# A weight gradient computed transposed: 240 matmuls of 512 columns for 384 of 320, with a round trip through DRAM to turn the result back

## The chip, the cores and the metric

The kernel runs on one core of a Trainium2 chip. The metric is device time in microseconds (us), from repeated executions; a profile of one execution gives a span that is about 2 us shorter than its time.

## The reference

A two-layer MLP with a SiLU in the middle, forward and backward, in bf16:

```python
B, S, D, F = 1, 2048, 640, 1536
def _fwd_reference(x, w1, w2):
    h = silu(einsum("bsd,df->bsf", x, w1))
    return einsum("bsf,fd->bsd", h, w2)
# outputs: out, and the gradients gx, gw1, gw2 for a given grad_out
```

The part of interest is gw2 = aᵀ · grad_out, with a = silu(x·w1): a matrix of 1536 x 640, summed over 2048 rows. gw1 is the same kind of product: xᵀ · gh.

## The kernel before

The main phase runs over four chunks of 512 rows. In each it makes `aT` and `ghT` (features on partitions), writes both to DRAM scratch, and computes `out` and `gx` from them. The final phase needs `a` and `gh` with rows on partitions, so it reads the scratch back through transposing DMAs. All DMAs are issued from SyncE, on one queue, in order. A matmul is written with a stationary operand (`lhsT`, put in place by a weight load) and a moving one (`rhs`), whose columns are counted below. Its sums go to PSUM tiles; an eviction is the copy of a finished tile from PSUM to on-chip memory by ScalarE or VectorE.

```python
    ps_h = ctx.enter_context(tc.tile_pool(name="ps_h", bufs=4, space=bass.MemoryType.PSUM))
    ps_o = ctx.enter_context(tc.tile_pool(name="ps_o", bufs=2, space=bass.MemoryType.PSUM))
    ...
    def load_a_blk(ft, pool):                       # one block of 128 features
        a_blk = pool.tile([P, ST, P], dt_in, name="a_blk")
        nc.sync.dma_start_transpose(out=a_blk[:], in_=aT_scr[ft * P:(ft + 1) * P, :])
        a_blks.append(a_blk)
    ...                                             # main phase; its last chunk loads blocks 0 to 3
        ab2pool = fctx.enter_context(tc.tile_pool(name="ab2pool", bufs=FT - NAB))
        for ft in range(NAB, FT):                   # blocks 4 to 11, in memory that the main phase frees
            load_a_blk(ft, ab2pool)
        for fc in range(NFC):                       # then three gh blocks of 512 features
            gh_blk = gbpool.tile([P, ST, FC], dt_in, name="gh_blk")
            nc.sync.dma_start_transpose(out=gh_blk[:], in_=ghT_scr[fc * FC:(fc + 1) * FC, :])
            ...
        for ft in range(FT):                        # gw2: 12 x 2 x 16 matmuls, 320 moving columns
            a_blk = a_blks[ft]
            op_ = ps_o.tile([P, 2, 512], FP32, name="op")
            for hf in range(2):
                for st in range(ST):
                    nc.tensor.matmul(op_[:, hf, 0:DH], lhsT=a_blk[:, st, :],
                                     rhs=go_nat[:, st, hf * DH:(hf + 1) * DH], ...)
            nc.scalar.activation(gw2_sb[:, ft, :]..., op_[:, :, 0:DH], ACT.Copy)
        nc.sync.dma_start(out=gw2..., in_=gw2_sb[:])
        for fc in range(NFC):                       # gw1: 3 x 5 x 16 matmuls, 512 moving columns
            ...
```

## Time and profile before

323.03 us, median of 3 runs (323.01 to 323.51). The page of the profile, first the busy time of engines, then rows of the timeline (each digit is the busy tenths of one of 40 slices), then the chain that ended last (what the end of the kernel waited for, followed backwards), by engine:

```profile
PE 316.2 (98%) x1926; PEld 188.5 (59%) x1944; DVE 99.1 (31%) x172; ACT 78.9 (25%) x136; POOL 0.7 (0%) x6
...
PE   8999999999999999999999999999999999999996
...
DMA  7999999998794020291020079909999996211111
...
PE 97%; DMA 1%; issue 0%; DVE 0%; DVEq 0%
```

TensorE (PE) is busy in every slice and is 97% of the chain. VectorE (DVE) and ScalarE (ACT) are at a third or less. The DMA engines have idle stretches, the last at the end, during gw1.

The groups of gw2 and gw1 (line, engine, operation, output and input; count; then busy us and mean ns of one; then idle time before):

```profile
L263 PE MATMUL op<-go_nat,a_blk 128*128 128x320 bf16 x384 | 52.3, 299 | 0.0
L302 PE MATMUL hp<-gh_blk,x_nat 128*128 128x512 bf16 x219 | 48.2, 379 | 0.3
L263 PEld LDWEIGHTS <-a_blk 128*128 128x128 bf16 x384 | 37.5, 98 | 14.7
```

The 299 and 379 ns are durations of overlapping instructions, not the rate. The rate is read from the chain in order of time (start us, length us, what):

```profile
214.43 52.16 PE op L263 x384
...
266.86 10.74 PE hp L302 x49
...
277.65 10.74 PE hp L302 x49
...
318.52 0.29 DVE g_2755 L295
```

gw2 is one piece of 52.16 us: 52.16 / 384 = 135.8 ns a matmul. The gw1 pieces are 49 recorded matmuls (one record of fifty is missing), and start 277.65 - 266.86 = 10.79 us apart: 215.8 ns a matmul. The spacing of starts is called the pitch below. The last line is the last eviction.

The DMA issues of the final phase, in order of time (start us, length us, line, kind, what):

```profile
193.06 10.97 SPq L73 DMA_TRANSPOSE a_blk<-aT_scr  x4
204.13 0.53 SPq L192 DMA_DIRECT2D out_dram<-o_sb  x1
214.46 2.01 SPq L73 DMA_TRANSPOSE a_blk<-aT_scr  x1
216.53 0.57 SPq L192 DMA_DIRECT2D out_dram<-o_sb  x1
217.15 19.33 SPq L73 DMA_TRANSPOSE a_blk<-aT_scr  x7
236.53 26.25 SPq L254 DMA_TRANSPOSE gh_blk<-ghT_scr  x3
```

The fifth block of a is issued only when the main phase's last matmul has freed its memory, and the queue is then full until 262.8 us.

### The profile page before, as it was taken

To read this page: it belongs to the slowest core of one execution; us is meant where nothing else is said; L and a number is where in the kernel's file an instruction comes from. 1 tells how busy PE (TensorE), PEld (TensorE's weight loads), DVE (VectorE), ACT (ScalarE), POOL (GpSimd) and SP (SyncE) were. 2 spreads that over 40 slices of the span, in tenths; PEclk is the share of its full clock that TensorE was granted. 3 is DMA by queue.
4 is the path that set the end of the run, shared out by engine and by line. 5 is a ranking of instruction groups with operands and counts; after the bars stand their busy time and mean duration, and the time that the engine had idled before them with its cause. 6 is when DMAs were issued, how large, how long until landed. Compare 5 with 4: busy or idle time off the path is not lost.

```text
span 321.2 us, 4386 instructions
## 1 busy us (share of the span) xinstructions
PE 316.2 (98%) x1926; PEld 188.5 (59%) x1944; DVE 99.1 (31%) x172; ACT 78.9 (25%) x136; POOL 0.7 (0%) x6
## 2 busy tenths in 40 slices
PE   8999999999999999999999999999999999999996
PEld 6467457544577644477754467777777775444443
DVE  1860553577501287800357740220000000110001
ACT  3961000455210155411044521001111111000100
POOL 0000000000000000000000000000000000000000
PEclk9999999999999999999999999999999999999999
DMA  7999999998794020291020079909999996211111
GB/s 235 318 191 200 220 274 241 363 289 274 213 290 137 6 78 0 78 316 67 17 82 0 0 254 245 239 17 236 226 218 213 266 219 211 85 38 44 35 42 41
DMA packets 113731, 52.32 MB, mean 163 GB/s; under 512 B 84144, under 2 KB 113712, under 8 KB 113712
## 3 DMA queue, kind: packets, MB, share of 16 engines
q1 hardware_dynamic: 113712, 52.04, 64.1%
q8 instruction: 15, 0.25, 0.3%
q14 instruction: 4, 0.03, 0.0%
HBM read 9.18 MB, written 21.76 MB: 96 GB/s over the span
## 4 chain that ended last, share of the span: by engine, by line
PE 97%; DMA 1%; issue 0%; DVE 0%; DVEq 0%
PE op L180 32%; PE op L263 16%; PE hp L163 16%; PE hp L144 16%; PE hp L302 15%; DMA x_nat<-in_x_dram 1%; PE hp L284 1%; PE tp L118 0%; DVE g_2755 L295 0%; DVEq L295 0%
## 5 line engine op out<-in xcount | busy, mean ns | idle before, releaser
L144 PE MATMUL hp<-xT,w_nat 128*128 128x512 bf16 x229 | 56.3, 379 | 0.6
L163 PE MATMUL hp<-goT,w2T 128*128 128x512 bf16 x238 | 56.8, 379 | 0.1
L180 PE MATMUL op<-w1T,ghT 128*128 128x320 bf16 x384 | 52.8, 299 | 0.0
L180 PE MATMUL op<-w_nat,aT 128*128 128x320 bf16 x384 | 52.8, 299 | 0.0
L263 PE MATMUL op<-go_nat,a_blk 128*128 128x320 bf16 x384 | 52.3, 299 | 0.0
L151 ACT ACTIVATE aT<-hp 128x512 bf16<-128x512 f32 x48 | 28.7, 597 | 83.0 <-PE hp L144 83.0
L302 PE MATMUL hp<-gh_blk,x_nat 128*128 128x512 bf16 x219 | 48.2, 379 | 0.3
L180 PEld LDWEIGHTS <-aT 128*128 128x128 bf16 x384 | 37.5, 98 | 15.3
L180 PEld LDWEIGHTS <-ghT 128*128 128x128 bf16 x384 | 37.5, 98 | 14.8
L263 PEld LDWEIGHTS <-a_blk 128*128 128x128 bf16 x384 | 37.5, 98 | 14.7
L163 PEld LDWEIGHTS <-w2T 128*128 128x128 bf16 x240 | 23.5, 98 | 28.2
L144 PEld LDWEIGHTS <-w_nat 128*128 128x128 bf16 x240 | 23.4, 98 | 27.8
L170 DVE SCALAR_TENSOR_TENSOR ghT<-ghT,hp 128x512 bf16<-128x512 bf16 x48 | 32.5, 682 | 16.2 <-PE hp L163 16.2
L191 DVE CAST o_sb<-op 128x640 bf16<-128x640 f32 x16 | 13.2, 825 | 78.6 <-PE op L180 78.6
L302 PEld LDWEIGHTS <-x_nat 128*128 128x128 bf16 x224 | 21.9, 98 | 26.3
L156 DVE SCALAR_TENSOR_TENSOR ghT<-aT,v 128x512 bf16<-128x512 bf16 x48 | 33.0, 687 | 0.6
L153 ACT ACTIVATE t<-hp 128x512 f32<-128x512 f32 x48 | 28.4, 592 | 0.0
L155 DVE TENSOR_SCALAR v<-t 128x512 bf16<-128x512 f32 x48 | 20.5, 427 | 20.5 <-ACT t L153 20.5
L189 ACT ACTIVATE o_sb<-op 128x640 bf16<-128x640 f32 x16 | 11.2, 703 | 49.1 <-PE op L180 49.1
L270 ACT ACTIVATE gw_sb<-op 128x640 bf16<-128x640 f32 x12 | 8.4, 704 | 56.8 <-PE op L263 56.8
L313 DVE CAST g_2475<-hp 128x512 bf16<-128x512 f32 x1 | 0.7, 690 | 58.2 <-PE hp L302 58.2
L90 PE MATMUL wp<-warm 128*128 128x128 bf16 x36 | 3.8, 304 | 1.0 <-DVE warm L85 1.0
(31 smaller groups left out, 26.2 us busy)
## 6 DMA issues: line engine op xcount, KB each, us to landing
aT_scr<-aT SPq DMA_DIRECT2D x4, 1536.0 KB, 6.3
ghT_scr<-ghT SPq DMA_DIRECT2D x4, 1536.0 KB, 9.6
out_dram<-o_sb SPq DMA_DIRECT2D x8, 640.0 KB, 4.4
x_nat<-in_x_dram SPq DMA_DIRECT2D x4, 640.0 KB, 5.4
go_nat<-in_grad_out_dram SPq DMA_DIRECT2D x4, 640.0 KB, 7.0
w_nat<-in_w_dram SPq DMA_DIRECT2D x2, 960.0 KB, 11.5
out_dram<-gw_sb SPq DMA_DIRECT2D x1, 1920.0 KB, 6.9
w_nat<-in_w_dram SPq DMA_DIRECT2D x2, 640.0 KB, 7.6
```

The lines of the kernel that those rows point to most:

```text
L144: nc.tensor.matmul(hp[:], lhsT=w1_nat[:, dt_, ft * P:(ft + 1) * P], rhs=xT[:, dt_, :], start=(dt_ == 0), stop=(dt_ == DT - 1),)
L151: nc.scalar.activation(aT[:, ft, :], hp[:], ACT.Silu)
L153: nc.scalar.activation(t[:], hp[:], ACT.Tanh, scale=0.5)
L155: nc.vector.tensor_scalar(out=v[:], in0=t[:], scalar1=-0.5, scalar2=0.5, op0=ALU.mult, op1=ALU.add)
L156: nc.vector.scalar_tensor_tensor(out=ghT[:, ft, :], in0=aT[:, ft, :], scalar=1.0, in1=v[:], op0=ALU.subtract, op1=ALU.mult)
L163: nc.tensor.matmul(gp[:], lhsT=w2T[:, dt_, ft * P:(ft + 1) * P], rhs=goT[:, dt_, :], start=(dt_ == 0), stop=(dt_ == DT - 1),)
L170: nc.vector.scalar_tensor_tensor(out=ghT[:, ft, :], in0=ghT[:, ft, :], scalar=1.0, in1=gp[:], op0=ALU.add, op1=ALU.mult)
L180: nc.tensor.matmul(op_[:, hf, 0:DH], lhsT=lhs_all[:, ft, sl * P:(sl + 1) * P], rhs=rhs_all[:, ft, hf * DH:(hf + 1) * DH], start=(ft == 0), ...
L189: nc.scalar.activation(dst, op_[:, :, 0:DH], ACT.Copy)
L191: nc.vector.tensor_copy(out=dst, in_=op_[:, :, 0:DH])
L263: nc.tensor.matmul(op_[:, hf, 0:DH], lhsT=a_blk[:, st, :], rhs=go_nat[:, st, hf * DH:(hf + 1) * DH], start=(st == 0), stop=(st == ST - 1),)
L302: nc.tensor.matmul(gp[:], lhsT=x_nat[:, st, dt_ * P:(dt_ + 1) * P], rhs=gh_blk[:, st, :], start=(st == 0), stop=(st == ST - 1),)
```

## The change

The intent: gw2 streams 320 columns a matmul, because 640 is split in two. With the operands swapped (grad_out stationary, a moving) it streams 512, as gw1 does, in fewer matmuls and fewer weight loads. The result is then gw2ᵀ, which is written to a DRAM scratch, read back through a transposing DMA and stored. Loads of a become three blocks of 512 features. Core of the diff, with cuts:

```diff
-    abpool = ctx.enter_context(tc.tile_pool(name="abpool", bufs=NAB))
+    abpool = ctx.enter_context(tc.tile_pool(name="abpool", bufs=1))
+    g2T_scr = dram.tile([D, F], dt_in, name="g2T_scr")
-    def load_a_blk(ft, pool):
-        a_blk = pool.tile([P, ST, P], dt_in, name="a_blk")
+    def load_a_blk(fc, pool):
+        a_blk = pool.tile([P, ST, FC], dt_in, name="a_blk")
 ...
-        fpool = fctx.enter_context(tc.tile_pool(name="fpool", bufs=1))
+        fpool = fctx.enter_context(tc.tile_pool(name="fpool", bufs=NFC))
 ...
+        for fc in range(NFC):
+            a_blk = a_blks[fc]
+            g2T = fpool.tile([P, DT, FC], dt_in, name="g2T")
+            for dt_ in range(DT):
+                gp = ps_h.tile([P, FC], FP32, name="hp")
                 for st in range(ST):
                     nc.tensor.matmul(
+                        gp[:],
+                        lhsT=go_nat[:, st, dt_ * P:(dt_ + 1) * P],
+                        rhs=a_blk[:, st, :],
 ...
+                if k % 2 == 0:
+                    nc.scalar.activation(g2T[:, dt_, :], gp[:], ACT.Copy)
+                else:
+                    nc.vector.tensor_copy(out=g2T[:, dt_, :], in_=gp[:])
+            nc.sync.dma_start(out=g2T_v[:, :, fc * FC:(fc + 1) * FC], in_=g2T[:])
+        def store_gw2(fc):
+            g2 = fpool.tile([P, FB, D], dt_in, name="g2")
+            nc.sync.dma_start_transpose(out=g2[:], in_=g2T_scr[:, fc * FC:(fc + 1) * FC])
+            nc.sync.dma_start(out=gw2_v[:, fc * FB:(fc + 1) * FB, :], in_=g2[:])
 ...                                                # gw1 loop:
+                if dt_ == DT // 2:
+                    store_gw2(fc)
```

## The prediction

> **What bounds the kernel now.** TensorE, end to end. The page's first part has PE busy 98% of the 321.2 us span, the chain that ended last is 97% PE, and the granted clock is 1.000 (cores view). In the chain in order of time the gw2 stage is one piece: 384 matmuls in 52.16 us, 135.8 ns each, from 214.43 us, waiting for nothing. In the gw1 stage behind it (512 moving columns) pieces of 50 matmuls start 10.79 us apart: 215.8 ns each. Weight loads (98 ns each) hide under both. VectorE (31%) and ScalarE (25%) are far from a limit.
>
> **TensorE.** The columns streamed are equal: 384 x 320 = 240 x 512. From the two pitches one column costs (215.8 - 135.8) / 192 = 0.4167 ns and one matmul 2.5 ns beside its columns. That agrees with the Trainium skill, page "TensorE: Matmul & The Clock Gate", section "Wait — 56ns, not 53.3ns?": N / 2.4 GHz + about 2.5 ns when warm. The new stage costs 240 x 215.8 = 51.8 us, 0.36 us less: 144 matmuls fewer at 2.5 ns. The 144 fewer weight loads (14 us of PEld) were hidden and give nothing. That 0.36 us is on the critical path and is the whole gain.
>
> **Added, off the path.**
> - Evictions: 15 of 128x512 (0.60 us ScalarE, 0.69 us VectorE) for 12 of 128x640 (0.70 us). A PSUM tile fills in 3.45 us and has four buffers: no stall.
> - Loads of a: three transposing DMAs of 2 MB for twelve of 0.5 MB. The gh loads have this form: about 8.75 us of queue time, 11.3 us to landing. The second block can be issued only when main-phase buffers come free, at about 214.5 us (queue's waits: so it was for the fifth small block). Estimate: it lands near 226 us, needed at 214.4 + 17.3 = 231.7. The third lands near 236, needed at 249; the gh blocks end near 262, as before.
> - gw2 round trip: 1.9 MB written, transposed back, stored. The queue issues in order, so the first two scratch writes wait behind the gh loads (to about 260 us); the third trip falls near 267 to 283 us, where the DMA engines are 21% busy (windows view). gw1 stores wait some us behind it; three g1 buffers and four of PSUM cover that. All is over some 35 us before the end; the last gw1 tile and its store are unchanged.
>
> **Prediction.** 323.03 - 0.36 = 322.7 us; range 322.0 to 323.7. Faster by over 2%: 0.01; within 2%: 0.97; slower by over 2%: 0.02.
>
> **What the profile would show.** Right: the chain still 97% PE; gw2 in one piece of about 51.8 us at 215.8 ns, gw1 starting 0.4 us earlier; PEld down from 59% to about 54%; no PE wait on DMA at block boundaries; the scratch transposes landed before 290 us; tail equal. Wrong: a PE wait of some us near 231.7 us for the second a block; idle PE in gw1 released by ScalarE or VectorE (gw1 stores held up in the queue); the chain ending on a DMA of gw2.
>
> **What would make it wrong.** The second a block landing over 6 us later than estimated (a wait on a later buffer, DMA engines shared with the output store); the transposing read of the scratch far slower than the 5.9 us that equal-sized transposes of x took; a lower granted clock.

## The result and the profile after

322.58 us, median of 4 runs (322.52 to 322.96), against 323.27 us of the kernel before in all its 4 runs. The ratio is 0.998, with a 95% interval of 0.9963 to 0.9997: within 2%, and 0.69 us between the medians. Ratios here are the mean time of one kernel's runs over that of the other's of the same rounds, so not quite the ratio of the medians quoted. Executions over 1.5% slower than the fastest of the same kernel are left out of the means.

The same parts of the page, after:

```profile
PE 317.0 (99%) x1800; PEld 174.9 (55%) x1800; DVE 104.0 (32%) x179; ACT 75.3 (23%) x132; POOL 0.7 (0%) x6
...
PE   8999999999999999999999999999999999999996
...
DMA  7999999997795020191020079809999999851011
...
PE 98%; DMA 1%; DVE 0%; issue 0%; DVEq 0%
```

Still TensorE from end to end. Weight loads went down by four points of the span, and the DMA row is busy for two slices more.

The group and the chain in order of time, after:

```profile
L266 PE MATMUL hp<-a_blk,go_nat 128*128 128x512 bf16 x240 | 52.0, 379 | 0.0
...
L266 PEld LDWEIGHTS <-go_nat 128*128 128x128 bf16 x240 | 23.5, 98 | 28.2
```

```profile
214.48 51.80 PE hp L266 x240
266.28 48.35 PE hp L314 x224
314.63 3.51 PE hp L296 x32
...
318.21 0.29 DVE g_2613 L307
```

gw2 takes 51.80 us, 0.36 us less than 52.16, and gw1 follows without a gap. The DMA issues of the final phase, after:

```profile
192.88 10.32 SPq L73 DMA_TRANSPOSE a_blk<-aT_scr  x1
203.29 0.53 SPq L192 DMA_DIRECT2D out_dram<-o_sb  x1
214.51 7.51 SPq L73 DMA_TRANSPOSE a_blk<-aT_scr  x1
222.07 0.57 SPq L192 DMA_DIRECT2D out_dram<-o_sb  x1
222.70 10.54 SPq L73 DMA_TRANSPOSE a_blk<-aT_scr  x1
233.28 25.43 SPq L253 DMA_TRANSPOSE gh_blk<-ghT_scr  x3
258.88 1.02 SPq L278 DMA_DIRECT2D g2T_scr<-g2T  x2
262.47 3.76 SPq L282 DMA_TRANSPOSE g_2327<-g2T_scr  x1
...
277.02 2.73 SPq L282 DMA_TRANSPOSE g_2533<-g2T_scr  x1
...
283.29 0.38 SPq L283 DMA_DIRECT2D out_dram<-g_2533  x1
```

The second block of a was issued at 214.51 us, and its issue-to-landing time in the view of that tile is 9.6 us: it was there at 224.1 us, needed at 214.48 + 80 x 0.2158 = 231.7. The first two gw2 tiles wait for the queue until 258.88 us, behind the gh loads, though the first was complete at about 232 us. The third trip ends near 287 us, over 30 us before the end.

**What was left over.** The medians differ by 0.69 us and the stage by 0.36. The profiles let one separate what the change did from what varies anyway. Call A the start of the first matmul on the chunk's data (the end of the twenty transposes of x at the start), B the start of gw2, and C the end of the last eviction. A is the start of this piece of TensorE's timeline, before and after:

```profile
6.35 5.99 PE L144 MATMUL hp<-xT,w_nat 128*128 128x512 bf16 x26
```

```profile
6.40 5.77 PE L144 MATMUL hp<-xT,w_nat 128*128 128x512 bf16 x26
```

| run | A | A to B | B to C |
|---|---|---|---|
| before | 6.35 | 208.08 | 104.38 |
| after | 6.40 | 208.08 | 104.02 |
| after, second profile | 6.86 | 208.08 | 104.02 |

From A to C nothing varies by more than 0.01 us between these runs, except for what the change did: 0.36 us. What varies lies outside. A went from 6.35 to 7.13 us over all the profiles, and the time from C to the end of the span from 2.29 to 2.56 us (the kernel with gw2 last, which ends differently, left aside). The spans of the first two profiles differ by 0.42 us: 0.36 from B to C, 0.11 less after C, and 0.05 more before A. One run of each comparison has a trace, so that the rest of the 0.69 us between the medians lies before A or after C too is inferred.

### The profile page after: what moved, and what is told of

It reads as the page before. It is cut to its first block, busy times and chain, and to the rows that moved or that the text cites. A ratio compares the mean times of both kernels' runs of the same rounds, so it can differ in the third digit from the quotient of the medians.

```text
span 320.8 us, 4127 instructions
## 1 busy us (share of the span) xinstructions
PE 317.0 (99%) x1800; PEld 174.9 (55%) x1800; DVE 104.0 (32%) x179; ACT 75.3 (23%) x132; POOL 0.7 (0%) x6
## 4 chain that ended last, share of the span: by engine, by line
PE 98%; DMA 1%; DVE 0%; issue 0%; DVEq 0%
PE op L180 33%; PE hp L144 16%; PE hp L266 16%; PE hp L163 16%; PE hp L314 15%; DMA x_nat<-in_x_dram 1%; PE hp L296 1%; PE tp L118 0%; DVE g_2613 L307 0%; DVEq L307 0%
## 5 line engine op out<-in xcount | busy, mean ns | idle before, releaser
L266 PE MATMUL hp<-a_blk,go_nat 128*128 128x512 bf16 x240 | 52.0, 379 | 0.0
L266 PEld LDWEIGHTS <-go_nat 128*128 128x128 bf16 x240 | 23.5, 98 | 28.2
L163 PEld LDWEIGHTS <-w2T 128*128 128x128 bf16 x240 | 23.5, 98 | 28.2
L191 DVE CAST o_sb<-op 128x640 bf16<-128x640 f32 x16 | 13.2, 825 | 78.6 <-PE op L180 78.6
L144 PEld LDWEIGHTS <-w_nat 128*128 128x128 bf16 x240 | 23.5, 98 | 27.7
L276 DVE CAST g2T<-hp 128x512 bf16<-128x512 f32 x7 | 4.8, 692 | 43.4 <-PE hp L266 43.4
L274 ACT ACTIVATE g2T<-hp 128x512 bf16<-128x512 f32 x8 | 4.8, 597 | 60.0 <-PE hp L266 60.0
## 6 DMA issues: line engine op xcount, KB each, us to landing
ghT_scr<-ghT SPq DMA_DIRECT2D x4, 1536.0 KB, 10.1
```

What stands on the lines that cost most here:

```text
L144: nc.tensor.matmul(hp[:], lhsT=w1_nat[:, dt_, ft * P:(ft + 1) * P], rhs=xT[:, dt_, :], start=(dt_ == 0), stop=(dt_ == DT - 1),)
L163: nc.tensor.matmul(gp[:], lhsT=w2T[:, dt_, ft * P:(ft + 1) * P], rhs=goT[:, dt_, :], start=(dt_ == 0), stop=(dt_ == DT - 1),)
L191: nc.vector.tensor_copy(out=dst, in_=op_[:, :, 0:DH])
L266: nc.tensor.matmul(gp[:], lhsT=go_nat[:, st, dt_ * P:(dt_ + 1) * P], rhs=a_blk[:, st, :], start=(st == 0), stop=(st == ST - 1),)
```

## The experiments

Eleven kernels ran. "Before" in a comparison is the old kernel on the same chip.

**The changed kernel again**, unedited, with five rounds.

> The changed kernel once more, for a sharper ratio. Theory (144 matmuls fewer at 2.5 ns, nothing else on the path): 0.36 us less than before, ratio 0.9989. Rival (part of the first 0.69 us between the medians comes from elsewhere): 0.7 us, ratio 0.998.

Measured: 323.03 us (322.49 to 323.33, 5 runs), before 323.32; ratio 0.9988, interval 0.9976 to 1.0. The ratio is within 0.0001 of the theory's 0.9989, but its interval also holds the rival's. The trace decides: A to B is as before, and B to C is again 104.02 us. In this run the start was what varied. Transposes of x, in the kernel before and in this kernel's second profile (durations as minimum, median and maximum in ns):

```profile
L118 PE MATMUL tp<-ident,x_nat x20: 215/220/230, 5.1 to 6.1; 128*128 128x128 bf16 x20
```

```profile
L118 PE MATMUL tp<-ident,x_nat x20: 219/311/311, 5.1 to 6.8; 128*128 128x128 bf16 x20
```

The twenty took 1.30 us in the first and 1.95 us in the second (timeline view). Five in a row early in the second stand as one piece of 0.74 us, so their starts are (0.74 - 0.31) / 4, about 107 ns, apart; seven in a row in the first stand as 0.55 us, (0.55 - 0.22) / 6, about 55 ns apart. The Trainium skill, page "TensorE: Matmul & The Clock Gate", section "What's actually happening", says that the array runs at half its clock until a window of about 3.4 us has been busy, that the window runs freely, and that the switch therefore falls at a different place from run to run. This agrees with what is seen here, where the switch falls before or within the transposes. It is read from durations: the granted clock of these slices is shown as 1.00 in all of these runs.

**One term at a time: columns for a matmul.** Two kernels compute gw2 as changed, but with shorter moving operands:

```diff
-                for st in range(ST):
-                    nc.tensor.matmul(gp[:], lhsT=go_nat[...], rhs=a_blk[:, st, :], ...)
+                for lo in range(0, FC, 256):          # and 128
+                    for st in range(ST):
+                        nc.tensor.matmul(gp[:, lo:lo + 256], lhsT=go_nat[...],
+                                         rhs=a_blk[:, st, lo:lo + 256], ...)
```

> The changed kernel with gw2 in 480 matmuls of 256 moving columns, all else equal. Theory (a matmul costs 0.4167 ns a column and 2.5 ns beside them, weight loads hidden): pitch 109.2 ns, gw2 stage in the chain 52.4 us against 51.8. Rival (the gain came from fewer weight loads, which show when the matmul gets near the 98 ns of a load): pitch clearly above 109.2 ns, stage above 53 us.

> The same with 960 matmuls of 128 columns. Theory: pitch 55.8 ns, gw2 stage 53.6 us, 1.8 us more than with 512 columns. Rival (loads set the pace): a load of 98 ns can't hide behind 56 ns, pitch near 98 ns, stage near 94 us.

The stage in the chain in order of time, with 256 columns and then with 128:

```profile
214.99 52.40 PE hp L267 x480
```

```profile
214.55 53.60 PE hp L267 x960
```

Both are the theory's numbers: 109.2 and 55.8 ns a matmul. (The single times, 323.71 and 324.46 against 323.15 us for before, carry the scatter of the start.) That the gain comes from weight loads too long to hide is ruled out. With 128 columns there are 960 loads of 98 ns in 53.6 us:

```profile
L267 PEld LDWEIGHTS <-go_nat 128*128 128x128 bf16 x960 | 53.7, 98 | 0.1
```

The loader is busy without a pause and still adds nothing to the pace. So its 98 ns is the length of one load, of which several overlap, and not the time between loads. One thing the runs can't separate: every matmul here has a load of its own, so the 2.5 ns belongs to the pair, and whether a matmul that keeps its weights would cost it too was not tested.

**The loads alone.** The kernel before with three big loads of a and the old matmuls:

```diff
-        a_blk = pool.tile([P, ST, P], dt_in, name="a_blk")
+        a_blk = pool.tile([P, ST, FC], dt_in, name="a_blk")
 ...
-                        lhsT=a_blk[:, st, :],
+                        lhsT=a_blk[:, st, fo:fo + P],   # fo = (ft % 4) * P
```

> The kernel before with the new loads of a alone: three transposing DMAs of 2 MB in place of twelve, gw2 still 384 matmuls of 320 columns. Theory: the loads are off the path, ratio to before 1.000 within 0.0005, gw2 stage 52.16 us, no PE wait at the block boundaries. Rival (fewer DMAs gave part of the gain): ratio 0.999 or less.

Measured: 323.48 us (322.98 to 323.92), ratio 1.0007, interval 0.9994 to 1.002. The ratio is 0.0002 outside the expected band of 0.0005 about 1, well inside its own interval. In the trace A to B is 208.08 us, gw2 is 52.16 us in one piece, B to C is 104.38 us. The loads contribute nothing.

**No round trip.** The transposed tiles are stored straight into gw2, whose content is then wrong (relative error 1.41 in that output; the other three are right):

```diff
-            nc.sync.dma_start(out=g2T_v[:, :, fc * FC:(fc + 1) * FC], in_=g2T[:])
+            nc.sync.dma_start(out=gw2_v[:, fc * FB:(fc + 1) * FB, :],
+                              in_=<g2T, flattened and cut in rows of D>)
 ...
-                if dt_ == DT // 2:
-                    store_gw2(fc)
```

> The changed kernel without the round trip: the transposed tiles are stored straight into gw2, so that output is wrong on purpose; same bytes stored, no scratch, no transposing DMA. Theory (the trip is hidden under gw1): the same time as the changed kernel, 322.6 us within 0.2. Rival (its delay of the gw1 stores or its DMA traffic costs something): 0.5 us or more faster than the changed kernel.

Measured: 323.33 us (323.15 to 323.54), which is 0.30 us above the changed kernel on the same chip (against before, ratio 1.0002, interval 0.999 to 1.0014), and so a miss of "within 0.2 of 322.6". The profiled run, at 323.54 us the slowest of the five, shows nothing of the trip: it has A = 7.13 us, the latest of all, and 2.50 us after C against 2.31, but 208.08 us from A to B and 104.02 us from B to C, equal to the changed kernel in both. The trip costs nothing, where it stands. (The other four runs have no trace; that they too are late before A or after C is inferred.)

**Where it stands.** gw1 first and gw2 last (with the first gh block loaded early in place of the first a block, and sixteen buffers for the gw1 tiles in place of three, so that they don't stall):

```diff
-        for fc in range(NFC):   # gw2, then gw1 with store_gw2(fc) inside
+        for fc in range(NFC):   # gw1, then gw2 with store_gw2(fc) at each block's end
```

> The changed kernel with gw1 computed first and gw2 last (the first gh block loaded early in place of the first a block, sixteen buffers for the gw1 tiles so that their stores can wait). Theory (the round trip costs nothing only because gw1 stands behind it): after the last matmul an eviction of 0.6 us, a scratch write of about 3.5 us, a transposing read of about 5.5 us and a store of about 3.4 us stand in line, 13 us against 2 us now: about 334 us, chain ending on these DMAs. Rival (the trip is cheap anywhere): below 326 us.

Measured: 333.24 us in one look, 10.1 us above before. The end of the timeline, from the last eviction on:

```profile
318.53 0.60 ACT L322 ACTIVATE g2T<-hp 128x512 bf16<-128x512 f32 x1 [6.31 <-PE hp L314]
319.15 0.37 SPq L326 DMA_DIRECT2D g2T_scr<-g2T  x1
322.47 2.90 SPq L301 DMA_TRANSPOSE g<-g2T_scr  x1
327.38 0.37 SPq L302 DMA_DIRECT2D out_dram<-g  x1
```

Write, transposing read and store stand in line from 319.15 us to the end of the span at 331.4. The trip that is free in front of gw1 costs some 10 us behind it.

**The buffers.** The same kernel with fewer buffers for g2T and g2:

```diff
-        fpool = fctx.enter_context(tc.tile_pool(name="fpool", bufs=NFC))
+        fpool = fctx.enter_context(tc.tile_pool(name="fpool", bufs=2))      # and bufs=1
```

> The changed kernel with two buffers in place of three for the gw2 tiles. Theory (the scratch writes queue behind the gh loads until about 259 us, so the third block's evictions wait for the first write to land near 265 us, while four PSUM tiles fill by 262.8 us): PE idle once for 2 to 3 us in the last third of gw2, time near 325.3 us. Rival (the buffers are a reserve, not needed): no idle PE, 322.6 us.

> The same with one buffer. Theory: the second block's evictions wait until the first scratch write lands near 264 us; four PSUM tiles are full at 245.6 us; PE idle about 18 us, perhaps 2 us more for a colder clock after it: 339 to 346 us. Rival: as before, below 326 us.

Measured: 324.01 us with two (325.3 expected) and 342.12 us with one (339 to 346 expected), before 323.15. TensorE in order of time, with two buffers (gw2's last two pieces):

```profile
214.75 48.51 PE L266 MATMUL hp<-a_blk,go_nat 128*128 128x512 bf16 x224
264.09 3.61 PE L266 MATMUL hp<-a_blk,go_nat 128*128 128x512 bf16 x16 [0.83 <-ACT g2T L274]
```

and with one:

```profile
214.36 31.24 PE L266 MATMUL hp<-a_blk,go_nat 128*128 128x512 bf16 x144
262.00 23.78 PE L266 MATMUL hp<-a_blk,go_nat 128*128 128x512 bf16 x96 [16.39 <-ACT g2T L274]
```

With two buffers the stall is there, in the predicted place (after 14 groups of 16 matmuls), but it is 0.83 us and not 2 to 3. What was mis-sized is the landing of the first scratch write: the expectation had it near 265 us; it landed 3.50 us after its issue, at 263.34. The changed kernel's own trace held the figure: there the three writes took 3.5 to 6.4 us, and the read that waits for the first was issued at 262.47, 3.6 us after the write. B to C is 105.01 us, 0.99 us more than with three buffers. With one buffer TensorE is idle for 16.39 us, and the 96 matmuls after it take 23.78 us in place of 96 x 0.2158 = 20.72. That second loss of 3.06 us is the clock: the granted clock of the run is 0.975, its row falls to 7, 5 and 7 tenths there, and the windows view has it at 0.50 from 252 to 266 us and at 1.00 from 268 us. The page named above, section "HAM oscillation — how this bites in real kernels", says that TensorE falls back to half its clock after idling for more than about 3.4 us; this trace agrees. So three buffers are no reserve: the first two tiles are held from about 232 and 249 us until the queue has issued the gh loads.

**The same trick elsewhere.** If 2.5 ns a matmul is all there is, it is also to be had in `out` and `gx`, which use 320 columns as well. Six of their eight phases (chunks 0 to 2) were computed transposed, each with its own trip:

```diff
+        def sdT_phase(c, mov_all, w_all, dst_v, scr, on_act):
+            oT = opool.tile([P, DT, SC], dt_in, name="oT", tag="o_sb")
+            for dt_ in range(DT):
+                gp = ps_h.tile([P, SC], FP32, name="hp")
+                for ft in range(FT):
+                    nc.tensor.matmul(gp[:], lhsT=w_all[:, ft, dt_ * P:(dt_ + 1) * P],
+                                     rhs=mov_all[:, ft, :], ...)
+                ...                                    # eviction to oT
+            nc.sync.dma_start(out=<scr, columns of chunk c>, in_=oT[:])
+            o_sb = opool.tile([P, STC, D], dt_in, name="o_sb")
+            nc.sync.dma_start_transpose(out=o_sb[:], in_=<scr, columns of chunk c>)
+            nc.sync.dma_start(out=dst_v[:, c * STC:(c + 1) * STC, :], in_=o_sb[:])
```

The tile oT shares two buffers with o_sb.

> The changed kernel with the same trick in six of the eight out and gx phases (chunks 0 to 2): 60 matmuls of 512 columns for 96 of 320, through a scratch and a transposing DMA. Theory: 216 matmuls fewer at 2.5 ns, 0.54 us less than the changed kernel if all six trips stay hidden, about 322.0 us, and 0.9 us less than before. Rival (the single queue, which also brings the next chunk's operands, makes TensorE wait): slower than the changed kernel by a microsecond or more, with PE waits at a chunk's start.

Measured: 324.07 us (322.58 to 328.04, 6 runs). The 328.04 us run is slow; the five fast ones have a median of 323.96 us, against 323.03 for the changed kernel on the same chip, and a ratio to before of 1.0023, interval 0.9994 to 1.0052. That leans to the rival's side, but the interval holds 1. The trace has the rival's wait. In the profiled run (323.19 us) A to B is 208.09 us, so that the 0.54 us are given back in full: this one phase of chunk 1 takes 13.49 us, from 97.40 to 110.89, against 60 x 0.2158 = 12.95. TensorE in chunk 1:

```profile
97.40 10.52 PE L201 MATMUL hp<-ghT,w1T 128*128 128x512 bf16 x47
108.31 2.75 PE L201 MATMUL hp<-ghT,w1T 128*128 128x512 bf16 x12 [0.39 <-DVE oT L211]
```

and the queue ahead of it:

```profile
92.33 11.46 SPq L109 DMA_TRANSPOSE goT<-in_grad_out_dram  x1
103.88 0.53 SPq L213 DMA_DIRECT2D oT_scr<-oT  x1
107.46 2.50 SPq L215 DMA_TRANSPOSE o_sb<-oT_scr  x1
```

It is the stall of the two-buffer experiment again: the write of the first tile waits behind an 11.46 us load for the next chunk, and the eviction of the next tile waits for the write. The slower unprofiled runs, 326.23 and 328.04 us with a granted clock of 0.995, have no trace; whether they are longer stalls of this kind, with a clock that falls in them as in the one-buffer run, or something else, stays open.

Two versions with a third buffer, the second one with the `out` phase of the last chunk transposed as well:

```diff
-            v = tpool.tile([P, SC], dt_in, name="v")
+            v = tpool.tile([P, SC], dt_in, name="v", bufs=2)      # makes the room
-        opool = mctx.enter_context(tc.tile_pool(name="opool", bufs=2))
+        opool = mctx.enter_context(tc.tile_pool(name="opool", bufs=3))
```

> The six transposed phases again, with three buffers in place of two for the tile tag that the transposed tile and the output tile share (room for it comes from one buffer less for a small tile that VectorE alone writes and reads). Theory (the stall of the first try was an eviction waiting for a scratch write queued behind the next chunk's loads; a third buffer takes that wait away): no PE wait on VectorE in chunk 1, from the first matmul of the main phase to the end 0.54 us less than the changed kernel, times steady, about 322.2 us. Rival (the six trips overload the one queue whatever the buffers): still PE waits and a scatter up to some us.

> The same with the out phase of the last chunk too (seven phases). Theory: a further 36 matmuls fewer, 0.09 us, if its trip ends before the second a block is issued near 214.5 us; 0.63 us less than the changed kernel. Rival: its trip delays the second or third a block past the 7 us of margin, and TensorE waits in gw2.

Measured with six phases: 322.97 us (322.7 to 323.13), ratio 0.9994, interval 0.9982 to 1.0007; with seven: 322.43 us (322.08 to 322.9), ratio 0.9977, interval 0.9964 to 0.9991; before 323.14 in both. The time of the first missed its 322.2 us, by its start and its end: A was 7.07 us against the changed kernel's 6.40, and from C on it took 2.56 us against 2.31. From A to B it took 207.54 us, which is 0.54 us less than before, and no PE wait on VectorE is left. With seven phases A was 6.72 us and A to B 207.46, 0.62 less. With the 0.36 us of gw2 that makes 0.98 us; 396 matmuls fewer at 2.5 ns are 0.99. The rival on the a blocks fails: gw2 and gw1 still take 104.02 us from B to C. This last version is the fastest by its median and by its trace. Against the changed kernel it was not timed in the same rounds; the two intervals, each against before, overlap.

## Why the prediction was right

- *"0.36 us is on the critical path and is the whole gain."* Shown. gw2 went from 52.16 to 51.80 us, A to B stayed at 208.08, and the time after C (2.42 us before, 2.31 after) is within its scatter. The measured median (322.58) is 0.1 us below the 322.7 forecast; that the time came so close is luck, as the same kernel's median was 323.03 us when it ran again and the kernel before had 323.03 to 323.32 us. The interval from B to C is what confirms the 0.36.
- *"One column costs 0.4167 ns and one matmul 2.5 ns."* Shown with two more sizes, at 256 and 128 columns, and in the transposed `out` and `gx` phases.
- *"The fewer weight loads were hidden and give nothing."* Shown in so far as even 960 loads in the stage add nothing beyond 2.5 ns a matmul; whether these 2.5 ns are the matmul's or its load's is not shown, and the gain is the same either way. PEld went from 59% to 55%, as forecast within a point.
- *"A PSUM tile fills in 3.45 us and has four buffers: no stall."* Held, but on the condition that the eviction has a tile to write to. The two- and one-buffer runs show that the third buffer of g2T was needed for it. The prediction listed the queueing of the scratch writes and did not draw this conclusion.
- *"It lands near 226 us, needed at 231.7."* It landed at 224.1. The third landed at 222.70 + 13.2 = 235.9, forecast 236.
- *"All is over some 35 us before the end."* The last gw2 store was issued at 283.29 us and landed 3.3 us later: 34 us before the end of the span. That it cost nothing because gw1 stood behind it is shown by the swapped order, 10.1 us above before.

## What to carry to other kernels

When TensorE is the limit and the columns stay equal, the gain of longer moving operands is the number of matmuls saved times the fixed cost read from two pitches in the trace, here 2.5 ns; work that out before paying for it with DRAM traffic. The round trip through DRAM was free here only with work behind it and with enough buffers to hold the tiles until the one in-order queue got to them. For differences under a microsecond, compare intervals between two events in the traces, past the clock's warm-up, rather than whole times.

## What the Trainium skill lacked or had wrong

- "TensorE: Matmul & The Clock Gate", section "Wait — 56ns, not 53.3ns?": nothing lacking in this section (only its formula was compared); it is right here, and to the digit also with a weight load before every matmul: 55.8, 109.2, 135.8 and 215.8 ns at 128, 256, 320 and 512 columns.
- "Perfetto Trace Analysis", section "Identifying the Most-Contended Engine", names the busy share of LDWEIGHTS, beside the share of the peak FLOPs, as a measure of how close TensorE is to its limit. Here it went from 59% to 55% for 0.36 us in 323. In the stage of 128 columns the loads were busy for all of the 53.6 us without setting the pace, and in the faster stage of 512 columns for 23.5 of 51.80 us; by itself this share told nothing of the headroom.
- "TensorE: Matmul & The Clock Gate", section "What's actually happening", gives the varying moment of the switch, and a cost of under 1% of a typical span, but not what it does to a comparison: here it moved the first data matmul between 6.35 and 7.13 us over the profiles (together with up to 0.4 us from the first load), 0.2% of the span and yet more than the effect under study. The profile's granted clock showed 1.00 in slices where the transposes took 311 ns and not 220.
- "DMA: Bandwidth & Descriptors" tells that all issuing queues share the DMA engines, but I found no warning there that a long issue holds up every later one on its queue: here the issues of the three gh loads held it for 25.43 us, and two finished tiles waited until 258.88 us, which costs 0.99 us with two buffers and 19.45 us with one.
